# New instruction orders from a written table, in a two-layer kernel of long convolution and SwiGLU

## The chip, the cores and the metric

The kernel runs on one core of one Trainium2 chip. The metric is the device time of one execution in microseconds (us). A core has five engines with a queue of instructions each: TensorE (PE, matmuls and transposes), ScalarE (ACT), VectorE (DVE), GpSimd (POOL) and SyncE (SP, which here only starts DMAs). Each engine takes its instructions strictly in the order of its queue, and an instruction that waits holds up all that stand behind it on its engine.

## The reference

Two layers, each made of a part A (a shifted product, a causal convolution as long as the sequence, a gate) and a part B (SwiGLU). The inputs are bfloat16; S = 2048 rows, D = 512 columns, F = 1792.

```
def _A_ref(q, k, v, shift_k, ssm_k, ssm_D):
    # k_shift[s] = sum over 4 taps t of k[s - 3 + t] * shift_k[:, 3 - t]
    kv = k_shift * v
    y = irfft(rfft(kv padded to 2S) * rfft(ssm_k padded to 2S))[:S]
    y = y + kv * ssm_D
    return q * y

def _B_ref(x, w_gate, w_up, w_down):
    return (silu(x @ w_gate) * (x @ w_up)) @ w_down

x = A_q
x = x + _A_ref(_layernorm(x), A_k, A_v, A_shift_k, A_ssm_k, A_ssm_D)
x = x + _B_ref(_layernorm(x), B_w_gate, B_w_up, B_w_down)
x = x + _A_ref(_layernorm(x), A_k, A_v, A_shift_k, A_ssm_k, A_ssm_D)
x = x + _B_ref(_layernorm(x), B_w_gate, B_w_up, B_w_down)
return x
```

The convolution y does not depend on x, so it is computed once and used by both layers.

## The kernel before, in words

**Tiling.** The sequence is cut into 4 blocks of 512 rows; a block lies on 128 partitions with 4 rows (r = 0 to 3) each. The FFN (part B) works in 16 units: layer, block, half of a block (256 rows). A unit needs zT, the normalised and transposed x of its half. It walks through 14 tiles of 128 hidden columns in groups of 4, 4, 4 and 2: up and gate matmuls (recorded at L958, traced as L310, pf<-zT,wu_sb and pf<-zT,wg_sb, 8 matmuls of 128x256 to a piece), ACT's Silu (sg, L965) and copy (ht, L969), DVE's product of the two (L972), and the down matmuls into pd (L985).

**Convolution.** It is done by block transforms. Matmuls with a table of sines and cosines (fwd) give the spectra H of the filter and X of kv (L310 through by_residue, L531, and at the start through direct, L457), ACT evicts them (L418), DVE multiplies spectra (for block 0 in single slots: t at L641, Z at L645; for later blocks L652 to L666), adds and subtracts them (m at L790, L539; H at L556 and L545; G at L580), and matmuls with the table inv bring them back (L796 for block 0), which ACT evicts (Yk, L716). kv comes from 16 small matmuls a row (L500), ACT's copy (ks, L513) and DVE's product (L514). The convolution of the next blocks is mixed into the FFN units.

**LayerNorm.** Of 256 rows at a time, it computes sums on DVE (L808 to L811) or on ACT (sum L827, negative mean nm L830, squares L833, variance plus epsilon ve L837). Then GpSimd raises ve to the power -1/2 with a tensor_tensor on two numbers a partition (rstd; L813 when DVE made ve, L839 when ACT made it). This is the power step of the change's title. Of 32 power steps 24 are at L813 and 8 at L839. After it come nmr = nm * rstd (L851 on ACT, L847 on DVE) and the normalised rows (L858 on ACT, L863 on DVE). The later products with the convolution result (L885, L886; at the start L902 to L907) make the new x; a second LayerNorm makes z. z is transposed by DMAs that SP starts (L892), except for the first unit, where TensorE transposes it (ptz, L919), ACT copies half 0 of zT (L924) and DVE half 1 (L922).

**PSUM.** It is divided into slots: ring pf has 4 (FFN pieces, and spectra at the start), pc 2 (convolution matmuls), pd 2 (down matmuls). A matmul group may start only when the group that used its slot before has been evicted.

**Order.** No queue is ordered by the program text. The class Plan records 1,569 operations by calls of add, in the order of the text: an operation's number is its place in this record. The table ORDER (from L51) holds one rank for each operation; Plan.order sorts the operations by rank, and hands out ring slots in that order, and Plan.issue emits them, so each engine's queue is the sorted list restricted to that engine. (Estimates of duration in Plan also set which slot a tile gets and how many filler matmuls, wm at L1253, are put in front of TensorE's early waits.) The FFN's first matmul group is operation 332; operation 107 is the first power step (layer 0, block 0, first half, L839), operation 230 the third (second half of the same block, L839). The two power steps that stand between and behind them, 217 and 242, are at L813.

## Time and profile before

| | us |
|---|---|
| median of 3 runs (346.98 to 347.27) | 347.1 |
| span of the profiled execution | 345.6 |
| TensorE busy in the span | 337.1 (98%) |
| VectorE busy | 283.0 (82%) |
| ScalarE busy | 253.6 (73%) |
| GpSimd busy | 46.5 (13%) |
| first FFN matmul starts | 35.58 |

The span runs from the first to the last recorded instruction of one profiled execution; 1.5 us of the median lie around it. Of the 16 DMA engines a quarter of the span is used (25.3% by the largest queue). In the profile an instruction's line is that of the code before; a row of the timeline gives start, duration, engine, line, operation, output and inputs, shapes and count, and in square brackets how long the engine stood idle ahead of it and what ended that.

### The profile page before, as it was taken

How to read it: one execution, taken by the hardware profiler on the slowest of the kernel's cores; microseconds unless marked ns; L12 is line 12 of the kernel's file. 1: busy time of each engine (PE TensorE's matmuls, PEld its weight loads, DVE VectorE, ACT ScalarE, POOL GpSimd, SP SyncE). 2: the span in 40 equal slices, each digit the busy share in tenths (PEclk: the TensorE clock that was granted, in tenths of full speed). 3: DMA queues.
4: the chain of work that ended last, by engine and by line, in shares of the span. 5: the costliest groups of instructions: out<-in, count | busy, mean ns of one | idle time of the engine just before them, and what ended most of it. 6: DMA issues, size and time to landing. Idle time of an engine off the chain costs nothing.

```text
span 345.6 us, 6557 instructions
## 1 busy us (share of the span) xinstructions
PE 337.1 (98%) x2580; PEld 248.8 (72%) x2612; DVE 283.0 (82%) x481; ACT 253.6 (73%) x503; POOL 46.5 (13%) x46
## 2 busy tenths in 40 slices
PE   8998999999999999999999999999999999999996
PEld 7655867858687767868587867767685868777784
DVE  7897999999999998999999999989998525526120
ACT  6889999989976657878899794569684645446361
POOL 4051111104110101111110000110401000001000
PEclk9999999999999999999999999999999999999999
DMA  7999204030111715010104102130101020101011
GB/s 282 334 306 336 51 14 63 15 93 1 32 31 29 172 40 144 13 34 2 31 3 122 32 0 62 31 93 1 32 0 34 30 32 0 32 0 21 11 47 46
DMA packets 42089, 22.96 MB, mean 66 GB/s; under 512 B 33861, under 2 KB 39882, under 8 KB 42058
## 3 DMA queue, kind: packets, MB, share of 16 engines
q1 hardware_dynamic: 41904, 22.47, 25.3%
q8 instruction: 20, 0.33, 0.4%
q14 instruction: 11, 0.09, 0.1%
q10 hardware_dynamic: 154, 0.07, 0.1%
HBM read 12.33 MB, written 2.10 MB: 42 GB/s over the span
## 4 chain that ended last, share of the span: by engine, by line
PE 92%; ACT 5%; POOL 2%; issue 1%; DVE 0%; ACTq 0%
PE pf L310 55%; PE pd L985 28%; PE ps L310 5%; POOL rstd L839 2%; PE ps L457 1%; PE wm L1253 1%; ACT H L418 1%; ACT n L858 1%; PE pt L476 1%; ACT Yk L716 1%; ACT ks L513 0%; ACT ht L969 0%; PE pt L365 0%; ACT sg L965 0%; ACT hs L486 0%
## 5 line engine op out<-in xcount | busy, mean ns | idle before, releaser
L310 PE MATMUL pf<-zT,wu_sb 128*128 128x256 bf16 x896 | 110.4, 273 | 0.9 <-ACT zT L924 0.7
L310 PE MATMUL pf<-zT,wg_sb 128*128 128x256 bf16 x896 | 110.6, 273 | 0.1
L985 PE MATMUL pd<-wd_sb,ht 128*128 128x512 bf16 (+1 forms) x442 | 100.6, 372 | 1.1
L310 PEld LDWEIGHTS <-wu_sb 128*128 128x128 bf16 x896 | 87.7, 98 | 16.6 <-issue 0.9
L310 PEld LDWEIGHTS <-wg_sb 128*128 128x128 bf16 x896 | 87.7, 98 | 15.4
L969 ACT CAST ht<-pf 128x512 bf16<-128x512 f32 x112 | 64.8, 589 | 30.7 <-PE pf L310 29.2
L965 ACT ACTIVATE sg<-pf 128x512 bf16<-128x512 f32 x112 | 65.6, 601 | 19.1 <-PE pf L310 17.2
L985 PEld LDWEIGHTS <-ht 128*128 128x128 bf16 x462 | 45.0, 98 | 45.2 <-DVE ht L972 0.9
L813 POOL TENSOR_TENSOR rstd<-ve,nhalf 128x2 f32<-128x2 f32 x24 | 27.7, 1153 | 204.5 <-DVE ve L811 204.5
L972 DVE TENSOR_TENSOR ht<-ht,sg 128x1024 bf16<-128x1024 bf16 (+1 forms) x64 | 39.0, 620 | 15.2 <-ACT ht L969 10.2
L1021 ACT CAST dn<-pd 128x512 bf16<-128x512 f32 x28 | 16.1, 590 | 24.1 <-PE pd L985 22.9
L808 DVE BATCH_NORM_STATS2 bnst<-xc 128x6 f32<-128x512 bf16 x48 | 31.7, 686 | 0.7
L1024 DVE TENSOR_TENSOR xc<-xc,dn 128x1024 bf16<-128x1024 bf16 x14 | 9.6, 686 | 18.6 <-ACT dn L1021 18.6
L839 POOL TENSOR_TENSOR rstd<-ve,nhalf 128x2 f32<-128x2 f32 x8 | 15.1, 1892 | 62.4 <-ACT ve L837 62.4
L652 DVE TENSOR_TENSOR t<-X,G 128x2048 bf16<-128x2048 bf16 x18 | 22.0, 1220 | 0.1
L656 DVE TENSOR_TENSOR t<-X,G 128x2048 bf16<-128x2048 bf16 x18 | 21.9, 1217 | 0.0
L418 ACT ACTIVATE X<-ps 128x512 bf16<-128x512 f32 x32 | 18.3, 604 | 1.8 <-PE ps L310 1.4
L885 DVE TENSOR_TENSOR n<-n,Yk 128x1024 bf16<-128x1024 bf16 x15 | 10.3, 689 | 5.8 <-ACT n L858 2.8
L664 DVE TENSOR_TENSOR t<-t,t 128x2048 bf16<-128x2048 bf16 x12 | 14.6, 1220 | 0.2
L666 DVE TENSOR_TENSOR Z<-Z,t 128x2048 bf16<-128x2048 bf16 x12 | 14.6, 1220 | 0.1
L418 ACT ACTIVATE H<-ps 128x512 bf16<-128x512 f32 x24 | 14.1, 609 | 0.7 <-PE ps L310 0.7
L310 PE MATMUL ps<-hs,fwd 128*128 128x512 bf16 x36 | 11.6, 379 | 1.1 <-ACT H L418 1.1
(108 smaller groups left out, 322.5 us busy)
## 6 DMA issues: line engine op xcount, KB each, us to landing
hn<-in_A_ssm_k_dram SPq DMA_DIRECT2D x4, 512.0 KB, 5.8
vt<-in_A_v_dram SPq DMA_DIRECT2D x4, 512.0 KB, 6.1
xc<-in_A_q_dram SPq DMA_DIRECT2D x4, 512.0 KB, 5.1
out_dram<-xc SPq DMA_DIRECT2D x15, 128.0 KB, 1.8
wg_sb<-in_B_w_gate_dram SPq DMA_DIRECT2D x1, 1792.0 KB
wu_sb<-in_B_w_up_dram SPq DMA_DIRECT2D x1, 1792.0 KB, 7.7
wd_sb<-in_B_w_down_dram SPq DMA_DIRECT2D x1, 1280.0 KB, 12.9
kn<-in_A_k_dram SPq DMA_DIRECT2D x1, 512.0 KB, 4.3
```

The costliest lines, as they stand in the source:

```text
L310: nc.tensor.matmul(o, lhsT=lhsT, rhs=rhs, start=(n == 0), stop=(n == len(terms) - 1))
L418: add("ACT", act(D), lambda: nc.scalar.activation(out=view(), in_=ps.t[:], func=ACT.Copy, scale=scale), r=[ps], w=[(buf, keys)], conv=conv)
L652: dve(n * D, lambda t1=t1, part=part: nc.vector.tensor_mul(out=t1.t[:], in0=x.t[:, sl, 0, :], in1=g.t[:, sl, part, :]), [(x, key(slots, (0 ...
L656: dve(n * D, lambda t2=t2, part=part: nc.vector.tensor_mul(out=t2.t[:], in0=x.t[:, sl, 1, :], in1=g.t[:, sl, 1 - part, :]), [(x, key(slots ...
L808: add("DVE", 0.6, lambda st=st, i=i: nc.vector.bn_stats(out=st.t[:], in_=xs[c].t[:, i, :]), r=[(xs[c], (i,))], w=[st])
L813: add("POOL", pw, lambda: nc.gpsimd.tensor_tensor(out=rstd.t[:], in0=ve.t[:], in1=nhalf.t[:].to_broadcast((P, n)), op=ALU.pow), r=[ve, nha ...
L839: add("POOL", PWA, lambda: nc.gpsimd.tensor_tensor(out=rstd.t[:], in0=ve.t[:], in1=nhalf.t[:].to_broadcast((P, n)), op=ALU.pow), r=[ve, nh ...
L965: add("ACT", act(D), lambda ps=ps, o=o, sg=sg: nc.scalar.activation(out=sg.t[:, o:o + 2, :], in_=ps.t[:], func=ACT.Silu), r=[ps], w=[(sg, ...
L969: add("ACT", act(D), lambda ps=ps, o=o, ht=ht: nc.scalar.copy(out=ht.t[:, o:o + 2, :], in_=ps.t[:]), r=[ps], w=[(ht, (o // 2,))], due=(uni ...
L972: dve(n * W, lambda sg=sg, ht=ht: nc.vector.tensor_mul(out=ht.t[:], in0=ht.t[:], in1=sg.t[:]), [sg], [ht], due=(unit, k / pairs, 0.0, "h"))
L985: nc.tensor.matmul((pds[o] if not cs.start else pds[HP]).t[:, cs], lhsT=ht.t[:, q, o * P:(o + 1) * P], rhs=wt["d"].t[:, ft, cs], start=(ft ...
L1021: add("ACT", act(D), lambda o=o: nc.scalar.copy(out=dn.t[:, o, :], in_=pds[o].t[:]), r=[pds[o]], w=[(dn, (o,))], due=(unit, 1.0, 3.0, "h"))
```

## The change

Only ORDER changes, nearly every rank of it. The recorded operations, their operands and their tiles are the same 1,569. From the new ranks follow new queues on all five engines, other slots for some tiles and other places for filler matmuls.

```diff
@@ -49,64 +49,64 @@
 X_PE = lambda l, c, h: (l, c, h) in {(0, 0, 0), (1, 3, 1)}
 RINGS = {}
 ORDER = [
-    0, 3, 66, 2, 4, 5, 16, 31, 1, 27, 22, 23, 28, 29, 8, 6, 7, 9, 10, 32, 12, 11, 13, 14, 15, 34, 33, 35, 54, 55, 56, 24, 36, 25, 38, 26, 43, 39, 40,
-    58, 60, 63, 72, 64, 68, 73, 74, 17, 42, 18, 44, 51, 49, 50, 20, 21, 41, 19, 37, 69, 62, 61, 46, 86, 84, 85, 30, 45, 59, 52, 53, 65, 67, 47, 48,
-    57, 159, 164, 165, 168, 172, 76, 81, 83, 87, 90, 82, 88, 97, 98, 99, 78, 80, 89, 91, 92, 77, 101, 102, 103, 104, 93, 94, 95, 123, 111, 139, 176,
...
+    0, 3, 36, 6, 4, 2, 10, 23, 1, 20, 7, 18, 56, 57, 5, 12, 8, 9, 13, 24, 17, 14, 15, 16, 19, 32, 40, 33, 59, 71, 100, 29, 54, 39, 52, 25, 37, 31, 35,
+    63, 65, 68, 83, 53, 60, 51, 70, 11, 27, 21, 38, 28, 26, 45, 42, 47, 34, 79, 58, 67, 69, 64, 30, 22, 66, 61, 44, 41, 48, 43, 50, 49, 55, 46, 75,
+    134, 136, 137, 164, 309, 215, 84, 91, 93, 94, 106, 77, 85, 88, 89, 105, 95, 96, 98, 99, 107, 62, 80, 81, 82, 103, 86, 92, 102, 145, 112, 147, 158,
...
```

What this makes of the queues, around power step 107 and power step 230 (numbers of the record, with what they are):

```
ACT, before: 106 ve | 165 hs, 138 X, 141 X, 147 X, 171 H, 177 H, 169 H | 109 nmr, 111 n, 108 nmr, 181 H, 110 n, 257 ks, ...
ACT, after:  147 X, 106 ve | 173 H, 141 X, 138 X, 167 hs | 108 nmr, 171 H, 169 H, 110 n, 109 nmr, 179 H, 111 n, 177 H, 257 ks, ...

DVE, before: 153 t, 152 t, 151 Z, 154 Z, 155 Z, 160 t, 184 m, 185 m, 156 t, 157 t, 161 t, 158 Z, 163 Z, 159 Z, 162 Z, 194 m, 195 m
DVE, after:  153 t, 151 Z, 152 t, 150 Z, 155 Z, 154 Z, 160 t, 184 m, 161 t, 185 m, 157 t, 156 t, 163 Z, 159 Z, 162 Z, 158 Z, 194 m, 195 m

ACT, before: 266 ks, 224 sum, 220 zT, 225 sum, 226 nm, 228 sq, 227 sq, 229 ve | 344 ht, 333 ht, 335 sg, 331 sg, 275 X, 337 ht, 359 ht | 232 nmr, 234 n, 231 nmr, 233 n
ACT, after:  266 ks, 220 zT, 224 sum, 275 X, 225 sum, 226 nm, 333 ht, 228 sq, 355 ht, 227 sq, 342 sg, 229 ve | 335 sg, 344 ht, 331 sg, 337 ht | 231 nmr, 232 nmr, 279 X, 234 n, 233 n

DVE, before: 249 m, 248 m, 252 H, 253 H, 250 H, 251 H, 255 G, 254 G, 338 ht, 267 vt, 295 t, 235 n
DVE, after:  249 m, 248 m, 253 H, 250 H, 251 H, 252 H, 267 vt, 254 G, 255 G, 294 t, 338 ht, 295 t, 235 n

PE, after the first zT, before: 332, 343, 330, 334, 336, 358, 356, 341, 365, 354 (FFN pieces), 270 X, ...
PE, after the first zT, after:  332, 354, 341, 343, 334, 330, 336, 352, 358 (FFN pieces), 272 X, 347 (FFN piece), 276 X, ...
```

A bar stands behind ve and ahead of the first user of its power step. The squares (sq) that feed ve 106 move too: operation 104 stood in front of 135 X and stands behind 144 X. TensorE's order in the stage before (spectra of block 0, transposes hs) is permuted, and so are VectorE's small steps in the first 14 us (ands for the table, dg, vt, ev). GpSimd's memset of kTb (L359) moves behind two of the diagonals dg (L1138), and its first two iotas change places. SP's load of the first part of wd_sb (L393) moves behind the load of the second part and behind the loads of xc (L385), hn (L341) and kTb (L353) for the next block. Behind these stages the queues of all later units are permuted in the same manner.

## The prediction

> **What bounds the kernel now.** I read the page's busy shares first, then the chain of waits in the first 36 us, then TensorE's, VectorE's and GpSimd's timelines there.

> ```profile
> PE 337.1 (98%) x2580; PEld 248.8 (72%) x2612; DVE 283.0 (82%) x481; ACT 253.6 (73%) x503; POOL 46.5 (13%) x46
> ```

> TensorE is busy for 98% of the span. In its timeline I found no idle stretch between 35.58 and 342.2 us that another engine ends (holes of 0.22 us, one matmul long, are missing records). The 3.4 us after its end are the last eviction and the output. So a new order can gain only in front of the first FFN matmul at 35.58; behind it, it can only lose. In front the chain runs through one power step:

> ```profile
> 20.48 0.20 ACT ve L837
> 20.68 0.07 issue
> 20.75 5.31 POOL rstd L839
> 26.08 0.30 ACT nmr L851
> ...
> 35.05 0.49 ACT zT L924
> 35.58 8.89 PE pf L310 x80
> ```

> The power step 107 takes 5.3 us on two numbers a partition. ACT, which queues behind nmr, then has no pause from 26.08 to zT, and TensorE waits for it several times:

> ```profile
> 29.61 0.38 PE L310 MATMUL ps<-hs,fwd 128*128 128x512 bf16 x1 [1.06 <-ACT H L418]
> ...
> 33.51 0.38 PE L310 MATMUL ps<-vt,fwd 128*128 128x512 bf16 x1 [0.44 <-ACT ks L513]
> 35.58 0.60 PE L310 MATMUL pf<-zT,wu_sb 128*128 128x256 bf16 x4 [0.71 <-ACT zT L924]
> ```

> **What a power step waits for.** The page's groups give the 24 steps at L813 a mean of 1,153 ns and the 8 at L839 one of 1,892 ns. The shortest is 0.69 us. I laid each against VectorE's instructions:

> ```profile
> 20.75 5.30 POOL L839 TENSOR_TENSOR rstd<-ve,nhalf 128x2 f32<-128x2 f32 x1 [13.99 <-ACT ve L837]
> 38.49 1.01 POOL L839 TENSOR_TENSOR rstd<-ve,nhalf 128x2 f32<-128x2 f32 x1 [5.17 <-ACT ve L837]
> 82.28 1.60 POOL L839 TENSOR_TENSOR rstd<-ve,nhalf 128x2 f32<-128x2 f32 x1 [1.57 <-ACT ve L837]
> 246.72 3.81 POOL L839 TENSOR_TENSOR rstd<-ve,nhalf 128x2 f32<-128x2 f32 x1 [5.79 <-ACT ve L837]
> ```

> The steps at L813 end 0.55 us after the first VectorE instruction over which they start. Those at L839 start at any point of VectorE's work, and three are long. Around the first, VectorE shows:

> ```profile
> 21.03 1.29 DVE L790 TENSOR_TENSOR m<-Z 128x1024 bf16<-128x1024 bf16 x2
> 22.24 1.89 DVE L641 TENSOR_TENSOR t<-X,G 128x1024 bf16<-128x1024 bf16 x3
> 24.05 1.43 DVE L645 TENSOR_TENSOR Z<-t,t 128x512 bf16<-128x512 bf16 x4
> 25.50 1.29 DVE L790 TENSOR_TENSOR m<-Z 128x1024 bf16<-128x1024 bf16 x2
> ```

> VectorE's two-input instructions follow each other without a pause (a row begins before the last one's tail has ended) until 25.47, where m waits 0.03 us for the Z just ahead of it: 26.05 - 25.48 = 0.57. So the step ended 0.57 us behind VectorE's first pause, not behind any of the nine boundaries before it. At 82.28 one boundary was passed over, at 246.72 two; both ended 0.55 us behind such a 0.03 us pause. In those three the request came in the 7th, 5th and 13th instruction of an unbroken run. Four steps at L839 whose request came in the 2nd or 3rd instruction of a run (38.49 is one) were let in at the next boundary, without a pause, so "only behind a pause" is not literally true. I take: in the 5th or later, held until the pause.

> [...]

> **The change, part by part.** No operation is added or removed, so everything is a question of waits. Spacings, start to start, from the rows of before: ACT eviction of 512 columns 0.485, copy hs 0.895, square 0.71 (0.85 with its accumulator read), n 0.72, nmr 0.19; VectorE 0.602 for 1024 columns, 0.335 for 512, 1.136 for 2048; TensorE 0.2155 for a 512-column matmul, 0.873 for an FFN piece, 0.88 for a ks group.

> *Start to 14.46 us.* I walked TensorE's new order in these prices: it stays dense and reaches the spectra of kv (L457) at the same 14.46. Zero; the permuted small steps of VectorE and ACT lie beside TensorE. If a table or dg came late, TensorE would wait, at most the 0.95 us that ACT idled there for TensorE.

> *Request of step 107.* TensorE's new order ends 144 X at 14.46 + 4.75 = 19.21. ACT sees it at 19.4, then 144 X (0.485), the square moved behind it (0.71), 147 X (0.485): ve starts at about 21.15, the power step 0.4 later, 21.55 (before 20.75).

> *VectorE there.* Its run starts at 17.9 and the 16 instructions to 158 Z take 9 x 0.602 + 7 x 0.335 = 7.6, to 25.5. The only pause is again m behind the Z that it reads (158, 194). It could pause earlier only by waiting for an X of ACT; by the sums 161 t, 157 t and 156 t come 0.30, 0.35 and 0.45 after theirs. At 21.55 VectorE is in the 8th or 9th of the run. By the rows above the step is held and ends at 25.5 + 0.55, about 26.05, **no gain**.

> *ACT behind it.* Four operations instead of seven stand between ve and nmr (2.35 us), so ACT idles from 23.7 to 26.05, against 1.56 before. Behind nmr now come 15 evictions instead of 13, two n, two nmr, and the sum 224 no more in front of zT: 15 x 0.485 + 1.44 + 0.38 = 9.1, so zT starts at 35.2 (34.94 before), and the first FFN matmul, 0.64 later, at F = 35.8. The same sum for before gives 8.98 against 8.86 in the rows. TensorE's work from 26.9 (192 waits for 171's slot, which is evicted behind nmr) is 20 x 0.2155 + 4 x 0.88 + 0.44 = 8.3, to 35.2, and VectorE's LayerNorm chain comes 0.45 later than before, both just hidden. **+0.2.**

> *Third power step, 230.* ACT behind zT: sum 224, 275 X, sum 225, nm, 333 ht, square, 355 ht, square, 342 sg, then ve; by the rows ve stands at F + 4.7 (before, at 38.12, F + 2.5), the step at F + 5.1. VectorE: 249 m begins at about F - 0.6, 248, then a 0.03 us pause, then 253, 250, 251, 252 H, 267 vt, 254 G, 255 G, 294 t, 338 ht, 295 t. Each of these has an instruction between it and what it reads, or reads what ACT ended before, so no pause; 295 ends at F - 0.6 + 2 x 1.136 + 4 x 0.602 + 0.335 + 3 x 1.136 + 0.602 + 1.136 = F + 9.55, where 235 must wait for n, which waits for this very step. The request falls in the 6th instruction of the run. Before, it came in the 3rd of its run and the step took 1.01. If held, it ends at E = F + 10.1. ACT, through with sg and ht at F + 6.9, stands at nmr until then. TensorE goes on with nine FFN pieces, 272 X and a tenth (10 x 0.873 + 0.2155 = F + 8.95) and then waits at 276 X, whose slot 279 X frees two operations behind nmr: it resumes at E + 1.05, and loses 0.83 more at 365, which waits for ACT's 348. Stall: E - F - 7.07 = 3.0. **+3.0**; nothing if the step is in by F + 6.5.

> ```profile
> 35.00:40.00 5.00, 4.42 (x41) 3.96 (x41) 4.93 (x7) 4.87 (x14) 1.01 (x1) 1.00 0.37 82
> ```

> In this row of the table of stretches (TensorE, weight loads, VectorE, ACT, GpSimd) VectorE and ACT are full before too; no slack takes a wait of 3 us up.

> *Moved transfers.* wd_sb's first part goes on SP's queue behind five loads. SP's last of these was issued by 35.25 before; the landing, some 5 us later by the issue table's rows for loads, is ahead of its first use at F + 12. Zero; if late, TensorE waits for what is missing. The x, hn and k loads that now pass it come earlier, which nobody waits for. GpSimd's memset and iotas lie in front of 14.46.

> *Later units.* The other six steps at L839 have their requests near pauses or ACT work behind them (419 has 0.97 us of evictions only, but a pause close by). The DVE-fed steps hold VectorE itself, so it pauses. Zero to +1, I take zero.

> Sum on the profiled execution: 345.6 + 0.2 + 3.0 = 348.8; with the 1.5 us that lie around the span, **350.3**, against the median of 347.1.

> **Rivals.**
> - *Both let in* (the other side, faster): each step enters at the end of the VectorE instruction running at its request. 107 ends at about 22.9, ACT reaches nmr at 23.7 instead of 26.07, and the chain behind moves up until TensorE's own work sets F at about 33.7: -1.9, 345.2. For it: 13 boundaries let a step in. Against: the nine passed over. It decides if a request in the 6th and 8th of a run is admitted.
> - *First held, third let in*: +0.2, 347.3. One boundary to pass, as at 82.28, is the weakest of the three cases.
> - *First let in, third held*: -1.9 + 3.0, 348.2.
> - *The first step is long because it is the first.* Its end lies 0.57 behind the pause, where others lie 0.55, so chance is not excluded. Then it takes 5.3 us wherever it stands: 21.55 + 5.3 = 26.85, 0.8 more: 348.1, and 351.1 if the third is held as well. [...]

> **How the numbers follow.** Both held 0.52; first held, third let in 0.16; first let in, third held 0.06; first call 0.06; both let in 0.20. Measurement can tell 0.2% (0.7 us) from no change. Faster: the both-let-in case and a little, 0.21. Same: 347.3, 0.16. Slower: the rest, 0.63. The range reaches from 345.0 (both let in, with 0.2 for its floor) to 351.8 (first call and third held, 351.1, with 0.7 for a late unit). The likeliest case alone: 349.3 to 351.0.

> **What would show it.** In the changed profile: power step 107 requested near 21.5 and ending near 26.05, just behind VectorE's first pause; ACT idle some 2.3 us there; F near 35.8. Then step 230 ending 0.55 behind a run that ends at 295 t, and TensorE idle for 2 us or more between F + 8 and F + 13. Wrong, if either step ends at a boundary inside a run, if VectorE pauses inside it because an X comes late by my 0.3 us margins (the step would then end near 22.9), or if TensorE shows waits behind 50 us.

## The result and the profile after

The changed order takes 348.92 us (median of 7 executions, 347.27 to 349.45) against 346.69 of the order before (7 executions, 344.91 to 347.27, the three of the table above among them); the ratio is 1.0055, 95% interval 1.0033 to 1.0078. It is slower, by 1.9 us from the ratio, where 350.3 and 3.2 us were forecast. The profiled execution shows less than that: a span of 346.0 us against 345.6.

Page of the changed kernel, busy time by engine:

```profile
PE 336.4 (97%) x2583; PEld 247.9 (72%) x2612; DVE 282.6 (82%) x481; ACT 252.8 (73%) x503; POOL 43.5 (13%) x46
```

Its chain of waits in front of the first FFN matmul (start, duration, what):

```profile
20.66 0.32 ACT ve L837
20.98 0.07 issue
21.06 4.49 POOL rstd L839
...
25.57 0.29 ACT nmr L851
...
35.09 0.62 ACT zT L924
...
35.76 0.27 PE pf L310
```

Power step 107 is still held, and the first FFN matmul starts 0.18 us later than before. That number hides a part of the loss: in this execution TensorE's spectra of kv (L457) begin at 13.95, and at 14.46 in the profile of before. Counted from there, the first FFN matmul comes after 21.81 us instead of 21.12, 0.69 later. (The start of the spectra lies between 13.55 and 15.53 in the 14 profiles; why is not shown.) GpSimd's timeline has the steps at L839 that the text needs:

```profile
21.06 4.48 POOL L839 TENSOR_TENSOR rstd<-ve,nhalf 128x2 f32<-128x2 f32 x1 [14.16 <-ACT ve L837]
...
40.78 1.07 POOL L839 TENSOR_TENSOR rstd<-ve,nhalf 128x2 f32<-128x2 f32 x1 [7.56 <-ACT ve L837]
...
193.28 4.44 POOL L839 TENSOR_TENSOR rstd<-ve,nhalf 128x2 f32<-128x2 f32 x1 [11.13 <-ACT ve L837]
...
247.87 3.21 POOL L839 TENSOR_TENSOR rstd<-ve,nhalf 128x2 f32<-128x2 f32 x1 [4.72 <-ACT ve L837]
```

The third power step (40.78) is let in after 1.07 us, and TensorE has no wait behind it. Another, 1266 at 247.87, is held for 3.21; ACT has nothing between its ve and its nmr, and TensorE's timeline shows the only new wait behind 36 us:

```profile
26.40 0.59 PE L796 MATMUL ps<-m,inv 128*128 128x512 bf16 x2 [2.31 <-ACT H L418]
...
252.11 1.03 PE L310 MATMUL pf<-zT,wu_sb 128*128 128x256 bf16 x8 [0.51 <-ACT ht L969]
```

The first of these two rows is the wait at 192 that the prediction names: TensorE stands still for 2.3 us because the eviction 171 that frees its slot queues behind the held step's nmr. In this execution TensorE makes the wait up before zT: its last matmuls ahead of the first FFN matmul start at 34.75, while ACT copies zT from 35.09 to 35.71. The 0.69 us come from ACT, whose work behind nmr takes from 25.57 to 35.09, 9.52 us. What the wait costs in other executions is the subject of the experiments. Of the 7 executions 3 have a mean granted clock of 1.000 and take 347.27 to 348.20 us; 4 have 0.995 and take 348.92 to 349.45.

### The profile page after: what moved, and what is told of

Read it like the earlier page. It is cut to its first block, busy times and chain, and to the rows that moved or that the text cites. A ratio compares the mean times of both kernels' runs of the same rounds, so it can differ in the third digit from the quotient of the medians.

```text
span 346.0 us, 6559 instructions
## 1 busy us (share of the span) xinstructions
PE 336.4 (97%) x2583; PEld 247.9 (72%) x2612; DVE 282.6 (82%) x481; ACT 252.8 (73%) x503; POOL 43.5 (13%) x46
## 3 DMA queue, kind: packets, MB, share of 16 engines
q1 hardware_dynamic: 41904, 22.47, 24.5%
## 4 chain that ended last, share of the span: by engine, by line
PE 89%; ACT 5%; POOL 2%; DMA 1%; issue 1%; DVE 0%; SPq 0%; POOLq 0%
PE pf L310 56%; PE pd L985 27%; PE ps L310 6%; POOL rstd L839 2%; DMA kn<-in_A_k_dram 1%; PE ps L457 1%; ACT H L418 1%; ACT jk L833 1%; ACT Yk L716 1%; ACT n L858 0%; ACT X L418 0%; PE pt L365 0%; ACT ht L969 0%; ACT ks L513 0%; ACT nmr L851 0%
## 5 line engine op out<-in xcount | busy, mean ns | idle before, releaser
L310 PE MATMUL pf<-zT,wu_sb 128*128 128x256 bf16 x896 | 109.9, 273 | 0.7 <-ACT ht L969 0.5
L310 PE MATMUL pf<-zT,wg_sb 128*128 128x256 bf16 x896 | 109.7, 273 | 0.0
L310 PEld LDWEIGHTS <-wu_sb 128*128 128x128 bf16 x896 | 87.6, 98 | 18.1 <-issue 1.5
L310 PEld LDWEIGHTS <-wg_sb 128*128 128x128 bf16 x896 | 87.7, 98 | 15.5
L965 ACT ACTIVATE sg<-pf 128x512 bf16<-128x512 f32 x112 | 66.7, 606 | 24.4 <-PE pf L310 20.5
L972 DVE TENSOR_TENSOR ht<-ht,sg 128x1024 bf16<-128x1024 bf16 (+1 forms) x64 | 39.3, 619 | 26.3 <-ACT sg L965 21.1
L813 POOL TENSOR_TENSOR rstd<-ve,nhalf 128x2 f32<-128x2 f32 x24 | 22.4, 934 | 205.4 <-DVE ve L811 194.1
L808 DVE BATCH_NORM_STATS2 bnst<-xc 128x6 f32<-128x512 bf16 x48 | 31.8, 685 | 0.7
L839 POOL TENSOR_TENSOR rstd<-ve,nhalf 128x2 f32<-128x2 f32 x8 | 17.4, 2179 | 64.7 <-ACT ve L837 64.7
L418 ACT ACTIVATE X<-ps 128x512 bf16<-128x512 f32 x32 | 18.7, 607 | 3.4 <-PE ps L310 2.9
L418 ACT ACTIVATE H<-ps 128x512 bf16<-128x512 f32 x24 | 14.1, 610 | 1.3 <-PE ps L310 1.3
L603 ACT ACTIVATE kc<-kTb,tapF 128x512 bf16<-128x512 bf16 x16 | 12.4, 786 | 0.5 <-DVE Z L545 0.5
```

What stands on the lines that cost most here:

```text
L310: nc.tensor.matmul(o, lhsT=lhsT, rhs=rhs, start=(n == 0), stop=(n == len(terms) - 1))
L418: add("ACT", act(D), lambda: nc.scalar.activation(out=view(), in_=ps.t[:], func=ACT.Copy, scale=scale), r=[ps], w=[(buf, keys)], conv=conv)
L808: add("DVE", 0.6, lambda st=st, i=i: nc.vector.bn_stats(out=st.t[:], in_=xs[c].t[:, i, :]), r=[(xs[c], (i,))], w=[st])
L813: add("POOL", pw, lambda: nc.gpsimd.tensor_tensor(out=rstd.t[:], in0=ve.t[:], in1=nhalf.t[:].to_broadcast((P, n)), op=ALU.pow), r=[ve, nha ...
L839: add("POOL", PWA, lambda: nc.gpsimd.tensor_tensor(out=rstd.t[:], in0=ve.t[:], in1=nhalf.t[:].to_broadcast((P, n)), op=ALU.pow), r=[ve, nh ...
L965: add("ACT", act(D), lambda ps=ps, o=o, sg=sg: nc.scalar.activation(out=sg.t[:, o:o + 2, :], in_=ps.t[:], func=ACT.Silu), r=[ps], w=[(sg, ...
```

## The experiments

Except in the kernels that keep the changed kernel's table as printed, the table is laid out in five lines less, so that L834 there is L839 here. All ratios are against the order before on the same chip.

**The changed order again.** No edit.

> The changed order once more, beside runs of the order before on the same chip. The profiled execution of the changed order is 0.4 us longer in its span than that of before, the medians are 2.2 us apart. Theory A (the loss is one of order): the ratio comes out at 1.001 to 1.002 where the granted clock of both is 1.000, from +0.2 in front (first FFN matmul at 35.8 against 35.58) and +0.5 at TensorE's wait near 252. Theory B (the third power step is let in in some executions and held in others, +3.0): spans of the changed order fall into two groups about 3 us apart at the same clock. Theory C (the granted clock): the executions at 0.995 are 0.5%, or 1.7 us, longer, and executions of the order before at 0.995 are so too.

Measured: 348.65 us, ratio 1.0051 (1.0033 to 1.0070). Five of 9 executions have a granted clock of 0.995 and a median of 349.60; four have 1.000 and 347.59, which is 0.85 above the order before and a ratio of 1.0025, a little more than Theory A has. All 22 of the order before lie at 0.998 or above, 346.37 to 347.15. The profile is of one at 0.995; its table of stretches (length, then TensorE, weight loads, VectorE, ACT and GpSimd busy, then the granted clock, the DMA share, GB/s):

```profile
24.00:27.00 3.00, 0.68 (x5) 0.33 (x5) 2.85 (x7) 0.83 (x3) 2.13 (x1) 1.00 1.04 389
27.00:29.00 2.00, 2.00 (x18) 1.78 (x18) 0.00 (x0) 2.00 (x5) 0.00 (x0) 0.63 1.11 356
29.00:31.00 2.00, 2.00 (x8) 0.77 (x6) 0.38 (x1) 1.57 (x3) 0.00 (x0) 0.52 1.07 387
31.00:33.00 2.00, 2.00 (x22) 1.40 (x21) 1.90 (x5) 1.31 (x3) 0.00 (x0) 1.00 1.90 204
```

and the same table of the changed kernel's first profile, whose mean clock is 1.000:

```profile
24.00:27.00 3.00, 0.69 (x8) 0.38 (x6) 2.25 (x5) 1.43 (x4) 1.53 (x1) 1.00 1.05 380
27.00:29.00 2.00, 2.00 (x22) 1.31 (x21) 0.36 (x1) 2.00 (x5) 0.00 (x0) 1.00 1.11 366
29.00:31.00 2.00, 2.00 (x22) 1.41 (x22) 1.90 (x5) 2.00 (x5) 0.00 (x0) 1.00 1.03 371
```

Both have the same wait (0.68 and 0.69 us busy in the 3 us from 24). In the one the granted clock is then 0.63 and 0.52 in two stretches of 2 us, and TensorE gets 8 matmuls done from 29 to 31 instead of 22; in the other it stays at 1.00. The trace's clock record has half the clock from 27.53 to 30.94, 3.41 us. Over 348 us that lowers the mean by 0.005, so a mean of 0.995 stands for one such fall. From the end of the wait to the first FFN matmul it is 27.00 to 37.71, 10.71 us, against 26.40 to 35.76, 9.36: **1.35 us** for the clock. Theory B falls: step 230 takes 1.08 here too, and the groups are 2 us apart, not 3. Theory C holds in its first half and fails in its second: the order before never shows it. The low clock comes with the new order.

**Only the front, only the rest.** The 239 operations that stand ahead of the first FFN matmul in both tables, and all others, ranked by different tables.

```diff
 front only:  - front: before   + front: after     rest: before
 rest only:     front: before   - rest: before   + rest: after
```

> The 239 operations that stand ahead of the first FFN matmul in both orders in their new order, all others in the order of before. Theory A: power step 107 ends behind VectorE's first pause at 25.5, first FFN matmul at 35.7 to 35.9, +0.2 against before, so within what can be measured; no wait of TensorE near 252. If the loss were in front, it would show here with +1 or more.

> The other way round: the 239 operations in front in the order of before, all others in the new order. Theory A: first FFN matmul at 35.6, TensorE's wait of 0.5 near 252 behind power step 1266 is there, +0.5 against before. Theory that the loss is in front: no difference from before.

Measured: the front alone 349.48 us, ratio 1.0067 (1.0049 to 1.0084), 5 of 6 executions at 0.995; in its profile the clock is 0.62 and 0.53 in the same stretches. The rest alone 346.65 us, ratio 1.0006 (0.9997 to 1.0015), none below 0.999, although TensorE's gap of 0.50 us near 252 is there. So the loss is in the front, against Theory A, and the wait near 252 is too small to be told in the time. The one execution of the front alone at a clock of 1.000 takes 347.54 us, 0.8 more than before: the new front costs something without the low clock too.

**Fillers in the wait.** 42 matmuls of 128 columns whose result nobody reads, in place of 2.

```diff
-if start < warm_until and start - t > 0.5:
+if o.n == 192 or start < warm_until and start - t > 0.5:
 ...
-n = int((start - max(t, 0.3) - 0.3) / 0.106)
+n = 42 if o.n == 192 else int((start - max(t, 0.3) - 0.3) / 0.106)
```

> The changed order with 42 filler matmuls of 128 columns in place of 2 in front of 192 (TensorE's 2.5 us wait near 24 to 26.9 us); their results are used by nothing. Theory K (the wait lets TensorE's granted clock fall to about half for some 4 us in many executions, and that is the +2 in the median): no execution at a granted clock of 0.995, first FFN matmul at 35.8 in the profile, median about 1 us less than the changed order's, 347.5 to 347.8. Theory L (the clock falls whatever TensorE does there): the same share of executions at 0.995 and the same median, 348.7.

TensorE's timeline, and two rows of the table of stretches:

```profile
25.39 2.51 PE L1253 MATMUL wm<-wz 128*128 128x128 bf16 x42
27.98 0.59 PE L796 MATMUL ps<-m,inv 128*128 128x512 bf16 x2
```

```profile
27.00:29.00 2.00, 1.93 (x30) 1.58 (x27) 0.86 (x2) 1.85 (x4) 0.11 (x1) 1.00 1.09 359
29.00:31.00 2.00, 2.00 (x17) 1.08 (x15) 0.75 (x2) 2.00 (x6) 0.00 (x0) 1.00 1.08 382
```

Measured: 12 of 12 executions at 0.999 or above; ratio 1.0028 (1.0009 to 1.0047). The median, 348.41, is higher than I wrote, but so was the order before on that chip (346.99, up to 349.03), so the ratio is what counts: about half of the loss is gone (the interval overlaps that of the changed order). The first FFN matmul of the profile comes at 37.34 and not at 35.8 as I wrote, because the spectra of kv begin at 15.53 there; counted from them it is 21.81, as in the changed order's first profile. So the fillers take the low clock away and leave the 0.69 us of ACT's work. Theory K holds for the clock.

**Evictions ahead of the held step's nmr.**

```diff
 ACT, changed order:
-167 hs, 108 nmr, 171 H, 169 H, 110 n
+167 hs, 171 H, 169 H, 108 nmr, 110 n
```

> The changed order with one operation moved: on ACT nmr 108 goes behind 171 H and 169 H, so the evictions that TensorE waits for no longer queue behind the held power step. Theory K: TensorE's wait of 2.5 us near 24 shrinks below 1 us, no execution at 0.995; ACT's idle time takes up two evictions, first FFN matmul at 34.6 to 35.3; median 346.6 to 347.2. If the wait were TensorE's own (a late input and not the slot), the wait stays.

TensorE's longest wait there:

```profile
28.31 0.38 PE L791 MATMUL ps<-m,inv 128*128 128x512 bf16 x1 [0.81 <-ACT H L413]
```

Measured: 346.96 us, ratio 0.9995 (0.9979 to 1.0012), all 12 executions at 0.999 or above, first FFN matmul at 34.62, 20.98 us behind the start of the spectra (21.81 in the changed order, 21.12 before). Step 107 takes 4.49 here as well. One operation moved on ACT takes both parts of the loss away, with the power step as long as ever.

**The changed order a third time,** because the fillers and the moved evictions had run on a chip on which the changed order itself did not run. This one met a chip of its own.

> The changed order a third time, on whatever chip it meets. Its executions so far were at a granted clock of 0.995 in 9 of 16, the 24 of the runs with fillers and with the evictions first in none, but those were on another chip. Theory K (TensorE's wait of 2.5 us near 24 brings the clock down, in about half of the executions): again a third to two thirds of the executions at 0.995, each 1.0 to 2.0 us longer than the rest. If the clock falls on one chip only: none at 0.995, median 347.5 to 347.8.

Measured: 348.69 us, ratio 1.0050 (1.0032 to 1.0068), 6 of 7 at 0.995, which is more than the two thirds that I wrote, and 1.3 to 2.6 us longer than the seventh; the clock is 0.71 and 0.50 in the profile's stretches from 27 to 31. Over the three runs of the changed order 15 of 23 executions are at 0.995, with a median of 349.27, and 8 at 1.000, with 347.59.

Why in some executions and not in others, the traces' clock records tell, laid beside the matmuls. In all 14 profiles every change of the clock lies on a grid of 3.41 us, counted from the clock's first rise, and a low clock behind that rise is half the clock. For each period of the grid I added up how long TensorE stood idle in it:

| profile | period | TensorE idle in it, us | clock in the period behind |
|---|---|---|---|
| changed order, second run | 24.11 to 27.53 | 2.32 | 0.50 |
| front only | 24.07 to 27.48 | 2.32 | 0.50 |
| changed order, third run | 24.42 to 27.83 | 2.31 | 0.50 |
| changed order, first run | 21.90 to 25.31 | 1.53 | 1.00 |
| the same | 25.31 to 28.72 | 1.09 | 1.00 |
| evictions first | 25.33 to 28.74 | 1.15 | 1.00 |
| order before | 27.42 to 30.84 | 1.06 | 1.00 |

In three profiles the wait lies whole within one period, and the clock is at half in the next. In the changed order's first profile the end of a period, at 25.31, cuts the wait in two, and the clock stays. Each profile, whatever its chip, has one more fall, behind the last matmuls, after a period with 2.02 to 3.41 us idle (such falls make the means of 0.998 and 0.999, and no matmul is left for them to slow). So all 17 periods with 2.02 us or more were followed by half the clock, and none with 1.53 or less; in between no profile has one. That the chip of the fillers and of the moved evictions does not lower its clock is thereby excluded: it does so at the end of all four profiles taken there.

**A pause behind the request.** 158 Z reads what 157 t writes.

```diff
 VectorE, order before:
-156 t, 157 t, 161 t, 158 Z, 163 Z
+156 t, 157 t, 158 Z, 161 t, 163 Z
```

> The order before with one operation moved: on VectorE 158 Z is put directly behind 157 t, which it reads, so that VectorE pauses 0.03 us at about 23.45 instead of only at 25.47. Theory H (held until a pause): power step 107 ends at 23.45 + 0.58 = 24.0, 2 us earlier; ACT, which is busy until 24.5, no longer idles 1.56 us, first FFN matmul at about 34.0, and the kernel 1.0 to 1.6 us faster. Theory F (the first power step takes 5.3 us because it is the first): it still ends at 26.05, no difference.

VectorE's and GpSimd's timelines:

```profile
22.36 1.29 DVE L636 TENSOR_TENSOR t<-X,G 128x1024 bf16<-128x1024 bf16 x2
23.68 0.43 DVE L640 TENSOR_TENSOR Z<-t,t 128x512 bf16<-128x512 bf16 x1
```

```profile
20.87 3.35 POOL L834 TENSOR_TENSOR rstd<-ve,nhalf 128x2 f32<-128x2 f32 x1 [14.13 <-ACT ve L832]
```

VectorE's second t ends at 23.65 and the next instruction waits 0.03; the step ends at 24.22, 0.57 later, 2 us earlier than before (3.35 against 5.30 us). First FFN matmul at 34.27, 19.69 behind the start of the spectra, 345.27 us, ratio 0.9966 (0.9952 to 0.9979). Theory H holds, and the first power step is not long for being the first.

**A pause ahead of the request.**

```diff
 VectorE, order before:
-154 Z, 155 Z, 160 t, 184 m, 185 m
+154 Z, 155 Z, 184 m, 160 t, 185 m
```

> The order before with one operation moved: on VectorE 184 m is put directly behind 155 Z, which it reads, so the 0.03 us pause falls at about 20.45, ahead of the request of power step 107 (20.8), and none comes after it until 25.5. Theory P (only a pause after the request lets a step in): it ends at 26.05 as before, no difference in time. Theory N (early in an unbroken run, up to the third instruction, the next boundary lets it in): it ends at 21.6, ACT no longer idles 1.56, first FFN matmul at about 34.3, 1.0 to 1.5 us faster.

```profile
20.27 1.06 POOL L834 TENSOR_TENSOR rstd<-ve,nhalf 128x2 f32<-128x2 f32 x1 [13.53 <-ACT ve L832]
```

The step is let in between two instructions of an unbroken run, the first and second behind the pause. First FFN matmul at 33.54, 19.56 behind the start of the spectra, 345.65 us, ratio 0.9954 (0.9933 to 0.9974). Theory P falls: no pause is needed if the run has only begun.

**Further moves, for the best version.** Sum 224 behind zT 220 on ACT, with either pause; and the changed order with 184 m directly behind 154 Z, then also with the nmr of step 1266 behind three evictions.

```diff
 ACT, both orders of before with a pause:
-266 ks, 224 sum, 220 zT
+266 ks, 220 zT, 224 sum
 VectorE, changed order:
-155 Z, 154 Z, 160 t, 184 m
+155 Z, 154 Z, 184 m, 160 t
 ACT, changed order, second move:
-1265 ve, 1268 nmr, 1267 nmr, 1339 ht, 1321 ht, 1328 ht
+1265 ve, 1339 ht, 1321 ht, 1328 ht, 1267 nmr, 1268 nmr
```

> The order before with 158 Z directly behind 157 t, as in the run with the pause at 157, and on ACT the sum 224 behind zT 220 instead of ahead of it. zT then starts as soon as its transposes are done, about 0.3 us earlier: first FFN matmul at 34.0 against 34.27, and 1.3 to 1.8 us faster than before. If ACT's evictions ahead of zT and not the sum set it, no further gain.

> The order before with two operations moved: 184 m directly behind 155 Z on VectorE, and the sum 224 behind zT 220 on ACT. The first alone gave a ratio of 0.9954; the second starts zT some 0.3 us earlier. Expected 0.9945 to 0.9955; if ACT's later pieces give the 0.3 back in the first FFN unit, as the wait of 0.6 near 36 in the run with the pause at 157 and zT first suggests, 0.9954 again.

> The changed order with one operation moved: on VectorE 184 m goes directly behind 154 Z, which it reads, so the only pause near there falls at about 20.0, ahead of the request of power step 107 (21.1), which then comes in the 2nd or 3rd instruction of a run. Theory N (early in a run the next boundary lets it in): it ends by 22.4, ACT reaches nmr at 23.3 without idling, TensorE's wait of 2.5 near 24 goes, first FFN matmul near 33.7 (35.76 in the changed order), no execution at 0.995, 1.0 to 1.8 us faster than before; of it 0.5 is lost again near 252. If the rule is the pause alone: held to 25.5, as in the changed order.

> The changed order with 184 m directly behind 154 Z, and on ACT the two nmr of power step 1266 behind the next three evictions ht instead of ahead of them. TensorE's wait of 0.5 to 0.7 us near 252, which the changed order has behind the held step 1266, goes, since its slots no longer queue behind it: 0.5 us faster than the run with the first move alone. If the wait is not ACT's queue behind the power step, it stays.

Measured: the earlier zT brings nothing that can be told (0.9954, 0.9936 to 0.9971, with the pause at 157; 0.9972, 0.9957 to 0.9987, with the pause ahead); the second is below what I wrote. Counted from the spectra the first FFN matmul comes 0.37 us earlier, but TensorE then waits 0.45 us near 37 for an eviction, so the gain is given back in the first FFN unit. The changed order with 184 moved: step 107

```profile
20.73 0.86 POOL L834 TENSOR_TENSOR rstd<-ve,nhalf 128x2 f32<-128x2 f32 x1 [13.84 <-ACT ve L832]
```

is let in at once, the wait at 24 is gone, first FFN matmul at 33.10 (19.47 behind the start of the spectra), no execution below 0.999, 345.43 us, ratio 0.9959 (0.9940 to 0.9977). With the second move TensorE's wait near 252 is gone from the trace and the time is 344.97 us, ratio 0.9944 (0.9922 to 0.9965), the fastest here; the step from 0.9959 lies within the intervals.

## Why the prediction was right in its sign, and where it failed

- **Step 107 held, no gain: right.** Requested at 21.06 (forecast 21.55), ended at 25.54 (26.05), 0.58 behind VectorE's first pause; the whole front ran 0.5 us early in this execution, TensorE's spectra of kv starting at 13.95 instead of 14.46, and with that both are on the forecast. ACT idled 2.23 us (2.35). The rival in which the step is long because it is the first ("first call" among the chances) is refuted by 3.35 and 0.86 us for the same step in other orders. (In the working, 9 x 0.602 + 7 x 0.335 is 7.8 and not 7.6; the rows of before have eight of each, and 7.6 is what they take.)
- **"+0.2" for ACT behind the step: met by luck.** The first FFN matmul came at 35.76 (35.8), but only because the front began 0.5 us early; counted from the spectra it is +0.69. The term that was too small is "9.1" for ACT from nmr to zT, which measured 9.52. The sum took ACT as never idle there, and it waits for VectorE once:

```profile
33.65 0.59 ACT L513 CAST ks<-ps 128x512 bf16<-128x512 f32 x1 [0.36 <-DVE vt L514]
```

- **"If held, it ends at E = F + 10.1", +3.0: wrong.** Step 230 was requested at F + 5.02 (forecast F + 5.1), in the 6th instruction of an unbroken run, and let in at the next boundary, without a pause, in all runs with this order. This was the rival "first held, third let in", and one of the signs that the prediction itself names for being wrong. What failed is the line that I drew, "in the 5th or later, held until the pause". The trace of before already spoke against it: it has eight steps at L839, the prediction lists seven, and the one left out was requested in the 15th instruction of a run and let in at the next boundary:

```profile
150.88 0.74 POOL L839 TENSOR_TENSOR rstd<-ve,nhalf 128x2 f32<-128x2 f32 x1 [7.29 <-ACT ve L837]
```

- **"TensorE's work from 26.9 … just hidden": right at full clock, and incomplete.** I had the wait of 192 in the sum and charged it only by the work behind it. In 15 of 23 executions (those with a mean clock of 0.995) it was also followed by half the granted clock for 3.41 us, which moves the first FFN matmul by 1.35 us in the profile. Nothing in the trace of before has a TensorE wait that long between its start and its end, so no row showed it; the guard that I should have set is a cost for the idle itself. The runs with fillers and with the evictions first show the cause: the same power step and no low clock.
- **"Moved transfers … zero" and "Later units: zero to +1, I take zero": not to be told from zero.** No TensorE wait for wd_sb appeared (its first part's own row is 8.8 us to landing before, not 5, and 4.6 after, where it is issued at 33.07, and so still in time). Step 1266 leaves TensorE 0.51 us idle near 252, which the time does not resolve (1.0006 for the rest alone, at most 1.0015).
- **The sum.** 0.69 in front, 1.35 x 15/23 = 0.9 for the clock, 0.2 for the rest by its ratio of 1.0006: 1.8 of the measured 1.9. The forecast of 3.2 had its sign and its size from a stall that did not come. That the kernel became slower all the same, by something near it, is luck: the loss came by two other ways from ACT's queue behind the step that was held.

What stays open is the rule by which a running series of VectorE instructions lets a power step in. Of the requests at L839, those in the first to fourth instruction behind a pause were let in at the next boundary (three times one that came within 0.1 us of the request was passed by). The one in the 5th (82.28 in the order before) was held to the next pause, and so were 107 in the 7th or later, and others in the 7th, 13th and 15th, past up to nine boundaries. A step that was passed over once, more than 0.1 us after its request, was never let in without a pause. That of step 230 in the 6th was let in, in every run, and so was that at 150.88 in the 15th; there the next VectorE instruction is a statistics instruction (L808) with a single input tile, and whether that matters is not shown. The index alone is therefore not the rule. What the traces have in common is the end: every step at L839 that was kept waiting ends 0.55 to 0.58 us behind the end of a VectorE instruction. That need not be the first to end after the request; for 107 in the order before it is the tenth.

## What to carry to other kernels

Read a held instruction by what queues behind it: the order before lives with a power step of 5.3 us, but in the new order the evictions behind its consumer on ACT left TensorE idle for 2.3 us. Put work that another engine waits for ahead of the consumer of an uncertain step; one such move took the ratio from 1.005 to 0.9995 with the step held as before, and a dependent pair of VectorE instructions placed just before or behind the request freed the step itself (0.9954 and 0.9966). When medians and a profile disagree, look at the granted clock of each execution before looking for the difference in the profile. And compare two profiles from an event at the start of the part in question, not from the span's start, which here moved by up to 2 us.
